# Strassen's seven half-size products for the down matmul of tiles 1 to 8, and column halves for attention, in a fused attention and feed-forward kernel

## The chip, the cores and the metric

The kernel runs on one core of one Trainium2 chip. The metric is device microseconds (us) of one execution. TensorE is called PE in the profile, its weight loads PEld, VectorE DVE, ScalarE ACT, GpSimd POOL, and SyncE SP. "Matmul of 256 columns" means that the moving operand has 256 columns.

Ratios are the mean time of one kernel's fast runs over the mean of the other's fast runs of the same rounds, so they are not quite the ratio of the medians that stand beside them. A run counts as slow when it is over 1.5% above the fastest of the same kernel, and is left out of the ratios. The granted clock is the share of TensorE's full clock rate that the trace says it was given.

## The reference

```python
# q, k, v: (8 batches, 8 heads, 576 positions, 64); pool = 8
k_p, v_p = mean of k, v over groups of 8 positions      # 72 keys per head
attn = softmax(q @ k_p.T / 8)                           # 576 x 72
x = (attn @ v_p), heads side by side                    # 4608 tokens x 512
h = x @ w_in                                            # 512 -> 2048, "up"
out = (h * cos(h)) @ w_out                              # 2048 -> 512, "down", float32
```

## The kernel before

Tokens go in nine tiles (0 to 8) of 512. A tile has an up stage (64 matmuls, with a cosine on ACT and a multiplication on DVE) and a down stage (64 matmuls of 512 columns). The attention of batch t + 1 is woven into the down stage of tile t, at fixed positions in the list of matmuls. It goes in units of four heads by 256 positions; the last 64 positions of a batch, for all eight heads, are "the rest". `obank` are the two PSUM banks that the down stage writes, `bank` three pairs of banks for the up stage and attention. POOL sums groups of eight keys and values for batches 2 to 7, in the down stages of tiles 1 to 5 and, for batch 2, around the end of tile 0.

Values and row sums of the softmax come out of one full-width matmul, because the weights hold 64 columns of values and 64 of ones:

```python
def values(b, u, pair, later=None):
    ...
    for i in range(nh):
        pj, hp = divmod(h0 + i, 2)
        nc.tensor.matmul(pair[:, hp, (i // 2) * n:(i // 2 + 1) * n],
                         lhsT=vz[b % 2][:, pj, 2 * hp:2 * hp + 2, :].rearrange("p a d -> p (a d)"),
                         rhs=ex[:, ex_col(u, i):ex_col(u, i) + n])
    ...                                            # Ln on 64 partitions, twice
    nc.scalar.activation(out=inv, in_=lnc, func=ACTF.Exp, scale=-1.0)
    ...                                            # tensor_mul on 64 partitions, twice

def down_mm(o, ms, fc):
    nc.tensor.matmul(o, lhsT=g_sb[:, fc, ms * 128:(ms + 1) * 128],
                     rhs=w_out_sb[fc // 4][:, fc % 4, :], start=(fc == 0), stop=(fc == FFCH - 1))

def pool_add(b, which):
    ...
    add = nc.gpsimd.tensor_tensor
    add(out=s, in0=x[:, :, 0:4, :], in1=x[:, :, 4:8, :], op=ADD)                      # 4.06 us
    add(out=s[:, :, 0:2, :], in0=s[:, :, 0:2, :], in1=s[:, :, 2:4, :], op=ADD)        # 2.35 us
    ...
```

The last 128 rows of tile 8 are done in pieces of 256, 128 and 128 columns (`last_chunk`), so that little is left after the last matmul.

The softmax here doesn't subtract the row's maximum and nothing guards it: scores larger than these inputs give would overflow.

## Time and profile before

The median of three runs was 302.38 us (302.17 to 302.52), the span of the profile 301.4 us.

| stage (from matmul starts in the trace) | us |
|---|---|
| up stage, tiles 1 to 8, each | 13.85 |
| down stage, tiles 1 to 6, each | 17.45 |
| down stage, tile 7, tile 8 | 14.41, 13.84 |
| last matmul's start to the end of the span | 3.71 |

PE is never idle from tile 0 to the last matmul, so each stage is as long as its matmuls. (A stage runs from its first matmul's start to the next stage's; tile 8's down stage to its last matmul's start.) The lines that show it stand in the prediction. In a line of a group, the columns are line, engine, operation, tiles, shapes and count, then busy time and the mean of one in ns, then the engine's idle time just before it and what ended it.

### The profile page before, as it was taken

What the parts mean: (1) busy time and instruction counts of PE and PEld (TensorE: products, weight loads), DVE (VectorE), ACT (ScalarE), POOL (GpSimd) and SP (SyncE); (2) the same over time, 40 slices, a digit from 0 to 9 for tenths busy, and PEclk for the clock granted to TensorE, in tenths of its full rate; (3) what the DMA queues carried; (4) which work ended last, traced back from release to release, by engine and by line L of the source; (5) the groups of instructions that cost most, each with busy time, mean ns of one, the idle gap of its engine ahead of it and who ended that gap; (6) DMA issues with size and microseconds to landing.
All of it is one profiled execution on the core that took longest, in us unless ns stands there. A gap on an engine that the chain in (4) does not pass through costs nothing.

```text
span 301.4 us, 4625 instructions
## 1 busy us (share of the span) xinstructions
PE 293.9 (97%) x1816; PEld 143.2 (48%) x1816; DVE 170.8 (57%) x212; ACT 205.7 (68%) x254; POOL 130.4 (43%) x93
## 2 busy tenths in 40 slices
PE   8789999999999999999999999999999999999995
PEld 3445544445544454445444544455444544444444
DVE  5448637465467446754666556654775477425712
ACT  3786798469876987688778886789668966605500
POOL 8463016984983398239913990389300000000000
PEclk9999999999999999999999999999999999999999
DMA  7999999639526961697079617791811130131023
GB/s 152 197 207 206 206 205 195 141 55 176 117 60 124 167 127 29 146 158 140 6 170 143 129 36 171 94 174 39 141 32 35 37 70 0 37 70 35 0 67 75
DMA packets 44165, 32.91 MB, mean 109 GB/s; under 512 B 22128, under 2 KB 39408, under 8 KB 44144
## 3 DMA queue, kind: packets, MB, share of 16 engines
q0 software_dynamic: 19744, 18.07, 38.3%
q1 hardware_dynamic: 24160, 14.42, 20.5%
q8 instruction: 14, 0.23, 0.3%
q10 hardware_dynamic: 240, 0.13, 0.2%
q14 instruction: 7, 0.06, 0.1%
HBM read 36.70 MB, written 9.44 MB: 153 GB/s over the span
## 4 chain that ended last, share of the span: by engine, by line
PE 93%; DMA 4%; POOL 1%; DVE 1%; issue 0%; POOLq 0%; DVEq 0%
PE bank L297 41%; PE obank L310 41%; PE bank L241 5%; DMA kv_st<-in_v_dram 4%; PE bank L211 3%; PE bank L328 1%; PE bank L165 1%; POOL q_b L84 1%; PE obank L157 0%; PE obank L280 0%; PE obank L192 0%; DVE xT L282 0%; DVE vz L167 0%; POOL kv_st L84 0%; DVE o_sb L316 0%
## 5 line engine op out<-in xcount | busy, mean ns | idle before, releaser
L310 PE MATMUL obank<-w_out_sb,g_sb 128*128 128x512 bf16 x560 | 131.4, 379 | 0.0
L297 PE MATMUL bank<-xT,w_in_sb 128*128 128x512 bf16 x576 | 126.6, 379 | 0.0
L304 ACT ACTIVATE cos<-bank,half_pi 128x1024 f32<-128x1024 f32 x72 | 79.3, 1113 | 59.5 <-PE bank L297 59.5
L307 DVE TENSOR_TENSOR g_sb<-bank,cos 128x1024 bf16<-128x1024 f32 x72 | 87.3, 1223 | 43.0 <-ACT cos L304 42.9
L297 PEld LDWEIGHTS <-w_in_sb 128*128 128x128 bf16 x576 | 56.1, 98 | 67.6 <-issue 1.6
L310 PEld LDWEIGHTS <-g_sb 128*128 128x128 bf16 x560 | 52.8, 98 | 56.5 <-issue 2.0
L252 DVE TENSOR_TENSOR xT<-bank,inv 64x512 bf16<-64x512 f32 (+1 forms) x72 | 45.3, 629 | 40.8 <-ACT inv L248 40.1
L141 POOL TENSOR_TENSOR kv_st<-kv_st 72x2048 f32<-72x2048 bf16 x12 | 48.7, 4058 | 33.9 <-DMA kv_st<-in_k_dram 33.9
L247 ACT ACTIVATE lnc<-bank 64x512 f32<-64x512 f32 (+1 forms) x72 | 39.2, 544 | 3.1 <-PE bank L241 1.7
L316 DVE COPY o_sb<-obank 128x512 f32<-128x512 f32 x35 | 23.6, 689 | 30.9 <-PE obank L310 30.5
L218 ACT ACTIVATE ex<-bank 72x1024 bf16<-72x1024 f32 (+1 forms) x40 | 35.0, 929 | 8.5 <-PE bank L211 8.4
L142 POOL TENSOR_TENSOR kv_st<-kv_st 72x1024 f32<-72x1024 f32 x12 | 28.2, 2349 | 1.0
L248 ACT ACTIVATE inv<-lnc 128x512 f32<-128x512 f32 (+1 forms) x36 | 21.0, 583 | 1.1
L241 PE MATMUL bank<-ex,vz 72*128 72x256 bf16 (+1 forms) x176 | 20.0, 243 | 0.0
L241 PEld LDWEIGHTS <-vz 72*128 72x128 bf16 x176 | 13.6, 97 | 9.6 <-DVE xT L252 0.5
L145 POOL TENSOR_TENSOR kp<-kv_st 72x512 bf16<-72x512 f32 x12 | 14.9, 1263 | 0.5
L211 PE MATMUL bank<-qT,kk 64*72 64x256 bf16 (+1 forms) x192 | 13.2, 252 | 0.0
L211 PEld LDWEIGHTS <-kk 64*72 64x72 bf16 x192 | 7.4, 109 | 9.9 <-issue 7.2
L285 ACT ACT_TABLE_LOAD x9 | 11.5, 1283 | 0.9 <-PEq L519 0.7
L499 POOL COPY gate<-kk 1x1 bf16<-1x1 bf16 x5 | 0.9, 179 | 25.7 <-DMA kk<-kp 25.7
L288 ACT ACT_TABLE_LOAD x9 | 11.5, 1283 | 0.2
L103 POOL DMA_DIRECT2D kv_st<-in_v_dram x6 | 5.0, 841 | 8.8 <-PE bank L165 8.8
(55 smaller groups left out, 93.1 us busy)
## 6 DMA issues: line engine op xcount, KB each, us to landing
out_dram<-o_sb SPq DMA_DIRECT2D x70, 128.0 KB, 2.4
kv_st<-in_v_dram POOLq DMA_DIRECT2D x8, 576.0 KB, 13.7
kv_st<-in_k_dram POOLq DMA_DIRECT2D x7, 576.0 KB, 7.6
q_b<-in_q_dram POOLq DMA_DIRECT2D x6, 576.0 KB, 9.9
w_in_sb<-in_moe_w_in_dram POOLq DMA_DIRECT2D x4, 512.0 KB, 14.5
w_out_sb<-in_moe_w_out_dram POOLq DMA_DIRECT2D x4, 512.0 KB, 18.1
q_b<-in_q_dram POOLq DMA_DIRECT2D x4, 288.0 KB, 13.0
g_sb<-in_k_dram SPq DMA_DIRECT2D x1, 576.0 KB, 3.7
```

Source lines behind the costliest of these rows:

```text
L141: add(out=s, in0=x[:, :, 0:4, :], in1=x[:, :, 4:8, :], op=ADD)
L142: add(out=s[:, :, 0:2, :], in0=s[:, :, 0:2, :], in1=s[:, :, 2:4, :], op=ADD)
L211: nc.tensor.matmul(pair[:Sp, bank, c:c + n].rearrange("p (g n) -> p g n", n=64), lhsT=kk[b % 2][half[r], h0 + i, 0:Sp], rhs=att["qT", b][h ...
L218: nc.scalar.activation(out=ex[:, 0:nh * n].rearrange("p (a n) -> p a n", a=2), in_=pair[:Sp, :, 0:nh * n // 2], func=ACTF.Exp, scale=scale ...
L241: nc.tensor.matmul(pair[:, hp, (i // 2) * n:(i // 2 + 1) * n], lhsT=vz[b % 2][:, pj, 2 * hp:2 * hp + 2, :].rearrange("p a d -> p (a d)"), ...
L247: nc.scalar.activation(out=lnc[half[1 - hp]], in_=pair[half[1 - hp], hp, 0:w], func=ACTF.Ln)
L252: nc.vector.tensor_mul(out=x_out(b, u, half[hp]), in0=cols(pair[half[hp], hp, :], u), in1=cols(inv[half[1 - hp]], u))
L297: nc.tensor.matmul(h[:, j, :], lhsT=w_in_sb[fc // 4][:, ki, (fc % 4) * 128:(fc % 4 + 1) * 128], rhs=xT[:, ki, t * TILE:(t + 1) * TILE], st ...
L304: nc.scalar.activation(out=cos, in_=h, func=ACTF.Sin, bias=half_pi[:, :1])
L307: nc.vector.tensor_mul(out=g_sb[:, 2 * fp:2 * fp + 2, :], in0=h, in1=cos)
L310: nc.tensor.matmul(o, lhsT=g_sb[:, fc, ms * 128:(ms + 1) * 128], rhs=w_out_sb[fc // 4][:, fc % 4, :], start=(fc == 0), stop=(fc == FFCH - 1))
L316: nc.vector.tensor_copy(out=o[:, 0:n], in_=ps)
```

## The change

The intent is fewer columns on PE. Tokens, the 2048 inner features and the 512 outputs are each cut in half, and Strassen's scheme gives the four output blocks from seven products instead of eight. A tile's down stage has 7 x 16 = 112 matmuls of 256 columns instead of 64 of 512. The price is sums: of `g` in every tile (`gs`, `gx`, `gd`), of the weights once after tile 0, and of the products. The column halves of attention put row sums and values of two heads into the two 64-column halves of the array, so that logarithm and multiplication need one instruction on 128 partitions each instead of two on 64; that is to make room on ACT and DVE.

```diff
 def pool_add(b, which):
-        add(out=s, in0=x[:, :, 0:4, :], in1=x[:, :, 4:8, :], op=ADD)
-        add(out=s[:, :, 0:2, :], in0=s[:, :, 0:2, :], in1=s[:, :, 2:4, :], op=ADD)
+        for h in range(0, H, 2):
+            add(out=s[:, h:h + 2], in0=x[:, h:h + 2, 0:4, :], in1=x[:, h:h + 2, 4:8, :], op=ADD)
+        for h in range(0, H, 4):
+            add(out=s[:, h:h + 4, 0:2, :], in0=s[:, h:h + 4, 0:2, :], in1=s[:, h:h + 4, 2:4, :], op=ADD)
 def values(b, u, pair, later=None):
...
+        cs, ao = pair[:, 0, 0:w], pair[:, 1, 0:w]
+        for out_of, weights in ((cs, lambda i: ones[:Sp, :]),
+                                (ao, lambda i: vz[b % 2][:, (h0 + i) // 2, i % 2, :])):
+            for i in range(nh):
+                hp = i % 2
+                nc.tensor.matmul(out_of[hp * 64:hp * 64 + 64, (i // 2) * n:(i // 2 + 1) * n], lhsT=weights(i),
+                                 rhs=ex[:, ex_col(u, i):ex_col(u, i) + n])
...
+    def put_weights():              # wx = B11 + B22, wy = B11 + B12, wz = -(B21 + B22), two parts each
+    def put_weights_in_place():     # B12 -= B22, B21 -= B11 (as w_out_sb then stands), two parts each
+    def put_gs(fp): ...             # behind every second up_g; gx and gd behind the products
...
+        products = [
+            (1, True, False, sides(g_sb, 0, 0), of(w_out_sb[0:2], 1)),
+            (0, True, False, sides(g_sb, 1, 1), of(w_out_sb[2:4], 0)),
+            (1, False, True, sides(gs, 0, 0), of(w_out_sb[2:4], 1)),
+            (0, False, True, sides(gs, 0, 1), of(w_out_sb[0:2], 0)),
+            (1, True, False, sides(gx, 0, 0), of(wx, 0)),
+            (0, True, True, sides(gd, 1, 0), of(wz, 0)),
+            (1, False, True, sides(gd, 0, 0), of(wy, 0)),
+        ]                            # the first entry is the output bank; False, True adds into it
...
+        behind = {n: [m3, *gxs[0:1]], 2 * n: [m4, *gxs[1:]], 3 * n: [c12, *gds[0:2]], 4 * n: [c21, *gds[2:]],
+                  5 * n: [m1], 6 * n: [c11], 7 * n: [c22]}          # n = 16 matmuls
...
+            if t == 1:
+                for put in put_weights_in_place():
+                    put()
...
+            for put in put_weights():          # after tile 0's down stage
+                put()
```

Left out are buffers that share space to make room, the order of the up matmuls (first and second half of the features in turn) and the positions of attention among 112 matmuls; in tile 7 the values of the rest stay at position 16.

More of the change, by code (lines that the diff above doesn't have):

```diff
@@ L64 @@
     g_sb = wpool.tile([128, FFCH, TILE], BF16, name="g_sb")
+    HF, HT, HM = FFCH // 2, TILE // 2, d_model // 2
+    gs = wpool.tile([128, HF, TILE], BF16, name="gs")
+    gd = wpool.tile([128, FFCH, HT], BF16, name="gd")
+    gx = wpool.tile([128, HF, HT], BF16, name="gx")
+    wx = [wpool.tile([128, 4, HM], BF16, name=f"wx{i}") for i in range(2)]
+    wy = [wpool.tile([128, 4, HM], BF16, name=f"wy{i}") for i in range(2)]
+    wz = [wpool.tile([128, 4, HM], BF16, name=f"wz{i}") for i in range(2)]
     SpA = -(-Sp // 16) * 16
@@ L68 @@
     kp2 = [wpool.tile([SpA, H, 2, D], BF16, name=f"kp2{i}") for i in range(2)]
-    vz = [wpool.tile([Sp, KCH, 4, D], BF16, name=f"vz{i}") for i in range(2)]
+    vz = [wpool.tile([Sp, KCH, 2, D], BF16, name=f"vz{i}") for i in range(2)]
+    half_sums = wpool.tile([Sp, H, POOL // 2, D], FP32, name="half_sums")
     banks = [psum.tile([128, 2, 512], FP32, name=f"bank{i}") for i in range(3)]
@@ L86, in kv_tile @@
     def kv_tile():
-        return kvst.tile([128, 2 * H * POOL * D], BF16, name="kv_st", tag="kv_st")
+        return kvst.tile([128, 2 * KCH * ROW * D], BF16, name="kv_st", tag="kv_st")
     def even_part(st, i):
@@ L100, in load_kv @@
     def load_kv(b, which, src):
-        st = kv_tile()[:Sp].rearrange("p (i h t d) -> p i h t d", i=2, h=H, t=POOL)
-        nc.gpsimd.dma_start(out=st[:, 0].rearrange("p h t d -> p h (t d)"),
+        st = kv_tile()[:Sp, 0:H * POOL * D].rearrange("p (h t d) -> p h t d", h=H, t=POOL)
+        nc.gpsimd.dma_start(out=st.rearrange("p h t d -> p h (t d)"),
                             in_=src[b].rearrange("h (p t) d -> p h (t d)", t=POOL))
@@ L125, in v_part @@
     def v_part(b):
-        return vz[b % 2][:, :, 0:4:3, :]
+        return vz[b % 2]
     def put_kk(b, ps, pj0, pj1, copy):
@@ L136, in pool_add @@
         st = staged.pop((which, b))
-        x = st[:, 0]
-        s = st[:, 1].rearrange("p h t d -> p (h t d)").bitcast(FP32).rearrange(
-            "p (h t d) -> p h t d", h=H, t=POOL // 2)
+        x, s = st, half_sums
         add = nc.gpsimd.tensor_tensor
-        add(out=s, in0=x[:, :, 0:4, :], in1=x[:, :, 4:8, :], op=ADD)
-        add(out=s[:, :, 0:2, :], in0=s[:, :, 0:2, :], in1=s[:, :, 2:4, :], op=ADD)
+        for h in range(0, H, 2):
+            add(out=s[:, h:h + 2], in0=x[:, h:h + 2, 0:4, :], in1=x[:, h:h + 2, 4:8, :], op=ADD)
+        for h in range(0, H, 4):
+            add(out=s[:, h:h + 4, 0:2, :], in0=s[:, h:h + 4, 0:2, :], in1=s[:, h:h + 4, 2:4, :], op=ADD)
         if which == "k":
@@ L230, in inverse_tile @@
     def inverse_tile(w):
-        lnc = asb.tile([128, 512], FP32, name="lnc", tag="lnc", bufs=1)
         inv = asb.tile([128, 512], FP32, name="inv", tag="inv", bufs=3)
-        return lnc[:, 0:w], inv[:, 0:w]
+        return inv[:, 0:w], inv[:, 0:w]
     def values(b, u, pair, later=None):
@@ L238, in values @@
         ex = att.pop(("ex", b, u))
-        for i in range(nh):
-            pj, hp = divmod(h0 + i, 2)
-            nc.tensor.matmul(pair[:, hp, (i // 2) * n:(i // 2 + 1) * n],
-                             lhsT=vz[b % 2][:, pj, 2 * hp:2 * hp + 2, :].rearrange("p a d -> p (a d)"),
-                             rhs=ex[:, ex_col(u, i):ex_col(u, i) + n])
-        w = nh * n // 2
+        w = nh * n // 2
+        cs, ao = pair[:, 0, 0:w], pair[:, 1, 0:w]
[5 more added lines that the diff above has]
+                                 rhs=ex[:, ex_col(u, i):ex_col(u, i) + n])
         lnc, inv = inverse_tile(w)
-        for hp in range(2):
-            nc.scalar.activation(out=lnc[half[1 - hp]], in_=pair[half[1 - hp], hp, 0:w], func=ACTF.Ln)
+        nc.scalar.activation(out=lnc, in_=cs, func=ACTF.Ln)
         nc.scalar.activation(out=inv, in_=lnc, func=ACTF.Exp, scale=-1.0)
         def mul():
-            for hp in range(2):
-                nc.vector.tensor_mul(out=x_out(b, u, half[hp]), in0=cols(pair[half[hp], hp, :], u),
-                                     in1=cols(inv[half[1 - hp]], u))
+            nc.vector.tensor_mul(out=x_out(b, u, slice(0, 128)), in0=cols(ao, u), in1=cols(inv, u))
         if later is None:
@@ L280, in values_then @@
             nc.tensor.matmul(ao[hp * 64:hp * 64 + 64, (i // 2) * n:(i // 2 + 1) * n],
-                             lhsT=vz[b % 2][:, pj, 3 * hp, :], rhs=ex[:, ex_col(u, i):ex_col(u, i) + n])
+                             lhsT=vz[b % 2][:, pj, hp, :], rhs=ex[:, ex_col(u, i):ex_col(u, i) + n])
         nc.vector.tensor_mul(out=x_out(b, u, slice(0, 128)), in0=cols(ao, u), in1=cols(att.pop(("inv", b, u)), u))
@@ L288, in sin_tables, with up_order, up_bank @@
         nc.scalar.preload_act_table_set("trig_and_small")
+    def up_order(t):
+        n = FFCH // 2
+        return range(n) if t == 0 else [i + a * n // 2 for i in range(n // 2) for a in range(2)]
+    def up_bank(t, fp):
+        return banks[list(up_order(t)).index(fp) % 3]
     def up_mm(t, fp, k0=0, k1=KCH):
-        h = banks[fp % 3]
+        h = up_bank(t, fp)
         for j in range(2):
@@ L301, in up_g @@
     def up_g(t, fp, between=()):
-        h = banks[fp % 3]
+        h = up_bank(t, fp)
         cos = msb.tile([128, 2, TILE], FP32, name="cos", tag="cos", bufs=2)
@@ L311, in down_mm, with down_out @@
                          rhs=w_out_sb[fc // 4][:, fc % 4, :], start=(fc == 0), stop=(fc == FFCH - 1))
-    def down_out(t, ms, ps, c0=0, queues=(nc.sync, nc.sync)):
-        o = msb.tile([128, d_model], FP32, name="o_sb", tag="o_sb", bufs=6)
-        n = ps.shape[1]
-        nc.vector.tensor_copy(out=o[:, 0:n], in_=ps)
+    def down_out(t, ms, ps):
+        o = msb.tile([128, 2, d_model], FP32, name="o_two", tag="o_two", bufs=3)[:, 0]
+        nc.vector.tensor_copy(out=o, in_=ps)
         rows_of = out.rearrange("(b p t) m -> b t p m", b=B, t=ROW)
@@ L319, in down_out @@
             b_, pos = divmod((t * TILE + ms * 128) // 64 + i, ROW)
-            queues[i].dma_start(out=rows_of[b_, ORDER[pos], :, c0:c0 + n], in_=o[rows, 0:n])
-    def last_chunk():
-        t, ms = NT - 1, 3
-        for i, (c0, n) in enumerate(((0, 256), (256, 128), (384, 128))):
-            ps = banks[i][:, 0, 0:n]
-            for fc in range(FFCH):
-                nc.tensor.matmul(ps, lhsT=g_sb[:, fc, ms * 128:(ms + 1) * 128],
-                                 rhs=w_out_sb[fc // 4][:, fc % 4, c0:c0 + n],
-                                 start=(fc == 0), stop=(fc == FFCH - 1))
-            down_out(t, ms, ps, c0, (nc.sync, nc.scalar))
@@ L334 @@
-    EX = 5
-    warm = consts.tile([128, 512], BF16, name="warm")
+            nc.sync.dma_start(out=rows_of[b_, ORDER[pos]], in_=o[rows])
+    def put_weights():
+        mul, sub = mybir.AluOpType.mult, mybir.AluOpType.subtract
+        for i in range(2):
+            (b11, b12), (b21, b22) = [(w[:, :, 0:HM], w[:, :, HM:]) for w in (w_out_sb[i], w_out_sb[i + 2])]
+            yield lambda i=i, x=b11, y=b22: nc.vector.tensor_tensor(out=wx[i], in0=x, in1=y, op=ADD)
+            yield lambda i=i, x=b11, y=b12: nc.vector.tensor_tensor(out=wy[i], in0=x, in1=y, op=ADD)
+            yield lambda i=i, x=b21, y=b22: nc.vector.scalar_tensor_tensor(out=wz[i], in0=x, scalar=-1.0, in1=y,
+                                                                          op0=mul, op1=sub)
@@ new lines, in put_weights_in_place @@
+    def put_weights_in_place():
+        sub = mybir.AluOpType.subtract
+        for i in range(2):
+            w1, w2 = w_out_sb[i], w_out_sb[i + 2]
+            yield lambda w1=w1, w2=w2: nc.vector.tensor_tensor(out=w1[:, :, HM:], in0=w1[:, :, HM:],
+                                                               in1=w2[:, :, HM:], op=sub)
+            yield lambda w1=w1, w2=w2: nc.vector.tensor_tensor(out=w2[:, :, 0:HM], in0=w2[:, :, 0:HM],
+                                                               in1=w1[:, :, 0:HM], op=sub)
@@ new lines, in put_gs, with put_gx, put_gd @@
+    def put_gs(fp):
+        f = slice(2 * fp, 2 * fp + 2)
+        nc.vector.tensor_tensor(out=gs[:, f], in0=g_sb[:, f], in1=g_sb[:, HF + 2 * fp:HF + 2 * fp + 2], op=ADD)
+    def put_gx(i):
+        f = slice(4 * i, 4 * i + 4)
+        nc.vector.tensor_tensor(out=gx[:, f], in0=g_sb[:, f, 0:HT], in1=g_sb[:, HF + 4 * i:HF + 4 * i + 4, HT:], op=ADD)
+    def put_gd(i):
+        f = slice(4 * i, 4 * i + 4)
+        nc.vector.tensor_tensor(out=gd[:, f], in0=g_sb[:, f, HT:], in1=g_sb[:, f, 0:HT], op=mybir.AluOpType.subtract)
@@ new lines, in down_products, with of, sides, m3 @@
+    def down_products(t):
+        def of(w, m):
+            return lambda fc: w[fc // 4][:, fc % 4, m * HM:(m + 1) * HM]
+        def sides(x, f, tk):
+            return lambda fc, p: x[:, f * HF + fc, tk * HT + p * 128:tk * HT + (p + 1) * 128]
+        products = [
[7 more added lines that the diff above has]
+        ]
+        mms = []
+        for bank, first, last, g, w in products:
+            for fc in range(HF):
+                for p in range(2):
+                    mms.append(lambda bank=bank, first=first, last=last, g=g, w=w, fc=fc, p=p: nc.tensor.matmul(
+                        obanks[bank][:, p * HM:(p + 1) * HM], lhsT=g(fc, p), rhs=w(fc),
+                        start=(first and fc == 0 and p == 0), stop=(fc == HF - 1 and p == 1), skip_group_check=not first))
+        e = msb.tile([128, d_model], FP32, name="e_sb", tag="e_sb", bufs=1)
+        u = msb.tile([128, d_model], FP32, name="u_sb", tag="u_sb", bufs=1)
+        os = [msb.tile([128, 2, d_model], FP32, name="o_two", tag="o_two", bufs=3) for _ in range(2)]
+        two = lambda x: x.rearrange("p (a m) -> p a m", a=2)
+        vec = nc.vector.tensor_tensor
+        sub = mybir.AluOpType.subtract
+        def m3():
+            nc.scalar.copy(out=e, in_=obanks[1])
+        def m4():
+            vec(out=e, in0=obanks[0], in1=e, op=ADD)
+        def c12():
+            nc.scalar.copy(out=os[0][:, :, HM:], in_=two(obanks[1]))
+            vec(out=u, in0=e, in1=obanks[1], op=sub)
+        def c21():
+            nc.scalar.copy(out=os[1][:, :, 0:HM], in_=two(obanks[0]))
+            vec(out=e, in0=e, in1=obanks[0], op=sub)
+        def m1():
+            vec(out=u, in0=obanks[1], in1=u, op=ADD)
+        def c11():
+            vec(out=os[0][:, :, 0:HM], in0=two(obanks[0]), in1=two(u), op=ADD)
+            rows_out(t, 0, os[0])
+        def c22():
+            vec(out=os[1][:, :, HM:], in0=two(obanks[1]), in1=two(e), op=ADD)
+            rows_out(t, 1, os[1])
+        gxs = [lambda i=i: put_gx(i) for i in range(2)]
+        gds = [lambda i=i: put_gd(i) for i in (2, 3, 0, 1)]
+        n = 2 * HF
+        behind = {n: [m3, *gxs[0:1]], 2 * n: [m4, *gxs[1:]], 3 * n: [c12, *gds[0:2]], 4 * n: [c21, *gds[2:]],
+                  5 * n: [m1], 6 * n: [c11], 7 * n: [c22]}
+        return mms, behind
@@ L336, with rows_out @@
+    def rows_out(t, tk, o):
+        rows_of = out.rearrange("(b p t) m -> b t p m", b=B, t=ROW)
+        for p in range(2):
+            for i, rows in enumerate(half):
+                b_, pos = divmod((t * TILE + tk * HT + p * 128) // 64 + i, ROW)
+                nc.sync.dma_start(out=rows_of[b_, ORDER[pos]], in_=o[rows, p])
+    EX = 4
+    warm = gx.rearrange("p f n -> p (f n)")[:, 0:512]
     nc.vector.memset(warm, 1.0)
@@ L357 @@
     make_identity(nc, identity)
-    dist = consts.tile([128, ROW, Sp], FP32, name="dist")
-    sign = consts.tile([128, ROW, Sp], FP32, name="sign")
-    groups = consts.tile([128, ROW, Sp], BF16, name="groups")
+    dist, sign = [gs.rearrange("p f n -> p (f n)").bitcast(FP32)[:, i * 1024:i * 1024 + ROW * Sp].rearrange(
+        "p (t n) -> p t n", t=ROW) for i in range(2)]
+    groups = gd.rearrange("p f n -> p (f n)")[:, 0:ROW * Sp].rearrange("p (t n) -> p t n", t=ROW)
     nc.vector.tensor_tensor(out=dist, in0=row_of.unsqueeze(2).to_broadcast([128, ROW, Sp]),
@@ L365 @@
     nc.vector.tensor_scalar(out=groups, in0=sign, scalar1=0.0, scalar2=None, op0=mybir.AluOpType.is_le)
-    nc.vector.memset(vz[0], float(POOL))
     ones = consts.tile([128, D], BF16, name="ones")
@@ L382 @@
     load_even(staged["v", 1], 1, v)
-    nc.gpsimd.memset(vz[1], float(POOL))
     for i in range(2):
@@ L427 @@
         if t > 0:
-            up_mm(t, 0, 0, 2)
-            up_mm(t, 1, 0, 2)
-        for fp in range(FFCH // 2):
-            up_mm(t, fp, 2 if fp < 2 else 0)
+            for fp in up_order(t)[0:2]:
+                up_mm(t, fp, 0, 2)
+            if t == 1:
+                for put in put_weights_in_place():
+                    put()
+        for n, fp in enumerate(up_order(t)):
+            up_mm(t, fp, 2 if n < 2 else 0)
             between = ()
@@ L443 @@
             up_g(t, fp, between)
+            if 0 < t and n % 2:
+                put_gs(n // 2)
             if 0 < t and b < B:
-                if fp == 0:
+                if n == 0:
                     q_transpose(b)
-                elif fp == 2:
+                elif n == 2:
                     k_transpose(b)
@@ L480, in scores_of @@
                 return go
-            fill = [(4, scores_of((b, us[0], 2), (b, us[1], 0))), (14, V_(0, 1, later)), (16, lambda: later.pop()()),
-                    (19, V_(1, 2)), (35, scores_of((b, us[2], 0), (b, us[3], 1), (t, REST, 2))),
-                    (38, V_(2, 0)), (43, lambda: values(t, REST, banks[1])), (46, V_(3, 2))]
+            fill = [(6, scores_of((b, us[0], 2), (b, us[1], 0))), (27, V_(0, 1, later)), (32, lambda: later.pop()()),
+                    (35, V_(1, 2)), (61, scores_of((b, us[2], 0), (b, us[3], 1), (t, REST, 2))),
+                    (67, V_(2, 0)), (76, lambda: values(t, REST, banks[1])), (82, V_(3, 2))]
         fi = 0
-        if t == NT - 1:
-            mms = mms[:-FFCH]
-        for n, (ms, fc) in enumerate(mms):
-            while fi < len(fill) and fill[fi][0] <= n:
-                fill[fi][1]()
-                fi += 1
-            down_mm(obanks[ms % 2], ms, fc)
-            if fc == FFCH - 1:
-                down_out(t, ms, obanks[ms % 2])
+        if t == 0:
+            for n, (ms, fc) in enumerate(mms):
+                while fi < len(fill) and fill[fi][0] <= n:
+                    fill[fi][1]()
+                    fi += 1
+                down_mm(obanks[ms % 2], ms, fc)
+                if fc == FFCH - 1:
+                    down_out(t, ms, obanks[ms % 2])
+            for put in put_weights():
+                put()
+        else:
+            mms, behind = down_products(t)
+            for n, mm in enumerate(mms):
+                for go in behind.get(n, ()):
+                    go()
+                while fi < len(fill) and fill[fi][0] <= n:
+                    fill[fi][1]()
+                    fi += 1
+                mm()
+            for go in behind[len(mms)]:
+                go()
         if t < B:
@@ L505 @@
             pool_add(b + 1, "v")
-    last_chunk()
 _INS = ['q', 'k', 'v', 'moe_w_in', 'moe_w_out']
```

## The prediction

No number of the sum goes with them: parts 1 to 6 come to +7.6 us, about 310, and 2 for contention with POOL make 312.

"Drain" is used below for the gap of 0.09 to 0.10 us that the prediction measures between matmuls on 128*128 and those on 64*72 or 72*64; what the array does in it was not shown.

> **What bounds the kernel now.** I read the page first (busy shares, then the chain that ended last), then the chain piece by piece, then short timelines of one tile.
>
> ```profile
> PE 293.9 (97%) x1816; PEld 143.2 (48%) x1816; DVE 170.8 (57%) x212; ACT 205.7 (68%) x254; POOL 130.4 (43%) x93
> PE 93%; DMA 4%; POOL 1%; DVE 1%; issue 0%; POOLq 0%; DVEq 0%
> L310 PE MATMUL obank<-w_out_sb,g_sb 128*128 128x512 bf16 x560 | 131.4, 379 | 0.0
> L297 PE MATMUL bank<-xT,w_in_sb 128*128 128x512 bf16 x576 | 126.6, 379 | 0.0
> L252 DVE TENSOR_TENSOR xT<-bank,inv 64x512 bf16<-64x512 f32 (+1 forms) x72 | 45.3, 629 | 40.8 <-ACT inv L248 40.1
> L247 ACT ACTIVATE lnc<-bank 64x512 f32<-64x512 f32 (+1 forms) x72 | 39.2, 544 | 3.1 <-PE bank L241 1.7
> ```
>
> TensorE (PE) carries 93% of the chain; up (L297) and down (L310) matmuls have no idle time before them. The two groups that the column halves shorten, Ln (L247) and the multiplication (L252), have slack: their engines are at 68% and 57%. So only a shorter PE stream, or a new wait on it, moves the time. The chain in order of time shows one tile (tile 2, from 85.46):
>
> ```profile
> 85.46 13.84 PE bank L297 x64
> 99.30 0.86 PE obank L310 x4
> 100.16 0.56 PE bank L211 x8
> ...
> 102.99 0.45 PE bank L241 x4
> ...
> 112.86 3.89 PE obank L310 x18
> 116.75 13.85 PE bank L297 x64
> ...
> 294.40 3.55 PE bank L328 x48
> ```
>
> Sixty-four matmuls of 512 columns take 13.84 us: 0.216 us each. Up plus down plus attention is 31.3 us a tile with no gap. The last line is the final chunk, 16 matmuls of 256 columns and 32 of 128, 3.55 us; its own starts are 0.109 and 0.056 us apart, so a new weight load of 128 columns hides even behind these short ones.
>
> [...]
>
> ```profile
> 99.35 0.81 PE L310 MATMUL obank<-w_out_sb,g_sb 128*128 128x512 bf16 x3
> 100.09 0.30 PE L211 MATMUL bank<-qT,kk 64*72 64x256 bf16 x2
> ...
> 12.19 0.41 PE L266 MATMUL obank<-ex,ones 72*64 72x256 bf16 x4 [0.15 <-DVE kk L132]
> 12.54 0.39 PE L392 MATMUL bank<-warm 128*128 128x512 bf16 x1
> ```
>
> The third matmul of the first line starts at 99.785, so a stream would go on at 100.00; the scores start at 100.09: 0.09 us. The column-half sums (L266) end their stream at 12.44 (last start 12.33 plus 0.107), the next full matmul starts at 12.53: 0.10 us. Within the mode a pair of halves takes 0.108 us, the first pair 0.03 more. [...] By analogy with L316 (128x512 f32, 0.69 us) I estimate a 1024-column bf16 sum at 0.69 us, 0.61 when it overlaps its predecessor (back-to-back L316 start 0.61 apart).
>
> **The change part by part.**
> 1. Down matmul: 64 x 0.216 = 13.81 us becomes 7 products x 8 x 2 = 112 matmuls of 256 columns x 0.109 = 12.23 us. Saved: 1.58 us in each of tiles 1 to 7; in tile 8, 48 x 0.216 + 3.55 - 12.23 = 1.68. Sum -12.8 us.
> 2. Column halves: a values unit is 4 x 0.109 = 0.44 us now. After it is 8 halves = 4 pairs, 0.43 + 0.03, plus 0.09 in and 0.10 out = 0.65: +0.21. The rest unit (8 x 64 columns) about +0.23. Four units and a rest in tiles 1 to 6: +1.07 each, 6.4; tile 0 about +1.0 (its rest follows another row-tiled group); tile 7 +0.23. Sum +7.6 us. Ln and multiplication halve on ACT and DVE, off the path.
> 3. The sums of the weights: ten DVE instructions between tile 0's last eviction (54.20 + 0.69 = 54.89, 0.73 after PE's end at 54.16) and tile 1's first multiplication by the cosine. At 0.61 to 0.69, perhaps 1.2 for the two three-operand ones: 6.3 to 7.4 us. DVE comes to that multiplication at 61.2 to 62.3, not 57.9. PE has three banks, so it stands when the fourth pair needs bank 0, at 54.16 + 3 x 1.73 = 59.35, and goes on 1.2 us after the multiplication starts, at 62.5 to 63.5. Sum about +3.5 us.
> 4. The end: the last product leaves a 128x512 combination (0.69 us against 0.29) and four output issues one after the other on one queue, at about 0.52 us each, behind the four of the other half; before, two small issues on two queues. Last matmul start to end of span is now 297.72 to 301.4, 3.7 us; I work out 6.4. Sum +2.75 us.
> 5. Waits in the down stage of tiles 1 to 6. Count from its start T (tile 2: 99.14).
>  - ACT: cosine to T+1.4, table load to 2.6, two exps to 3.65 and 4.56 (from 101.76 and 102.69 of tile 2). The new copy of product 1's bank stands behind them and ends at 5.15. PE reaches product 3, which adds into that bank, at 32 x 0.109 + 0.65 (scores) + 0.65 (values) + 0.1 = T+4.85: waits 0.3.
>  - Product 4's bank is copied by ACT behind three exps of scores that start at T+9.2: these take 2.87 us from the scores' start (108.34 to 111.20), so the copy ends at 12.6 and DVE's subtraction behind it at 13.4. PE wants that bank for product 6 at 13.2: 0.2.
>  - DVE, held by that subtraction with nothing running from about 10.7, then has two of the differences of g, two multiplications and the addition of product 5, which must be done before product 7 uses the bank: T+16.2 against T+15.8: 0.4.
>  Sum 0.9 x 6 = +5.4 us. In tile 7 the rest values stay at position 16, now T+2.1, but their exp ends at T+3.25 (258.25 + 0.59, T = 255.62): +1.15.
> 6. The new DVE sums in the up stage: 8 x 1.22 + 4 x 0.69 = 12.5 us of 13.8; fits.
>
> PE stream -12.8 + 7.6 = -5.2; plus 3.5 + 2.75 + 5.4 + 1.15 = +12.8. Net +7.6: about 310.
>
> **Rivals.**
> - *POOL contention.* POOL's sums run right through the down stage in tiles 1 to 5 and through the weight sums:
>
> ```profile
> 102.76 4.06 POOL L141 TENSOR_TENSOR kv_st<-kv_st 72x2048 f32<-72x2048 bf16 x1 [5.48 <-DMA kv_st<-in_k_dram]
> 106.91 2.35 POOL L142 TENSOR_TENSOR kv_st<-kv_st 72x1024 f32<-72x1024 f32 x1
> 109.34 2.49 POOL L145 TENSOR_TENSOR kp<-kv_st 72x512 bf16<-72x512 f32 x2
> 111.79 4.06 POOL L141 TENSOR_TENSOR kv_st<-kv_st 72x2048 f32<-72x2048 bf16 x1
> ```
>
>  The change cuts L141 into four and L142 into two, some 1.0 to 1.2 us each[...]. If DVE waits once per burst (about 0.55 us): product 7's wait grows by 0.5 in five tiles and the weights by 0.5, +3: 313. If the engines alternate, each DVE sum waits 1.1 us: product 7 waits 1.6 more in five tiles and the weights up to 7 more, +15: 325. I add 2 to the middle.
> - *The waits are absorbed.* If ACT and DVE come 0.5 us earlier than I laid out in a chain of a dozen steps, part 5 falls to 1 or 2 us: about 305. For it: the positions 27, 32 and 61 look fitted to when the exps end.
> - *The full saving comes through* (12.8 us, 4%, time 291). Against it: drains of 0.09 and 0.10 us are in the trace, as is the three-bank limit on a late DVE.
>
> **Range and chances.** Middle 310 + 2 = 312. Low end 304: parts 1 to 4 alone give 303.5. High end 322: contention between the two forms. Faster by over 2% needs under 296.3, below what parts 1 to 4 allow: 0.03. Within 2% ends at 308.4 and needs most of part 5 to vanish: 0.27. Slower: 0.70.
>
> **What would show it.** Right: starts of down matmuls 0.109 us apart in tiles 1 to 8; attention units of about 0.65 us; PE idle of 3 us or more, released by DVE's cosine multiplication, once after tile 0; PE waits before products 3, 6 and 7 in tiles 1 to 6, released by ACT's copy and DVE's subtraction and addition; bf16 sums longer than 0.69 us wherever POOL adds. Wrong: PE still without idle in tiles 1 to 6 (part 5 falls), a start spacing over 0.109 (weight loads not hidden), or bf16 sums near 1.2 us everywhere[...].

## The result, and the profile after

The changed kernel took 328.44 us median (327.24 to 328.64, 4 runs), beside 302.45 us (302.17 to 302.70) before: ratio 1.0849, 95% interval 1.0828 to 1.0869. It is slower by 26 us, outside the predicted range of 304 to 322.

| stage | before | after | difference |
|---|---|---|---|
| start to the end of tile 0 | 54.0 | 54.3 | +0.3 |
| tile 1, up | 13.85 | 27.72 | +13.9 |
| tile 1, down | 17.45 | 19.49 | +2.0 |
| tiles 2 to 5, down | 17.45 each | 19.06, 18.93, 19.72, 19.36 | +7.3 |
| tile 6, down | 17.45 | 17.59 | +0.1 |
| tile 7, down | 14.41 | 14.13 | -0.3 |
| tile 8, down | 13.84 | 12.12 | -1.7 |
| up stages of tiles 2 to 8 | 13.85 each | 13.84 each | 0 |
| last matmul to the end | 3.71 | 7.16 | +3.4 |

The page of the changed kernel, in the lines that answer to those shown of before:

```profile
PE 293.6 (90%) x2344; PEld 177.9 (55%) x2344; DVE 237.6 (73%) x279; ACT 196.3 (60%) x242; POOL 152.6 (47%) x140
PEclk9999999758999999999999999999999999999998
PE 24%; ACT 2%; DVE 1%; issue 1%; ACTq 0%
L314 PE MATMUL bank<-xT,w_in_sb 128*128 128x512 bf16 x576 | 128.9, 383 | 11.6 <-DVE g_sb L324 11.6
L367 DVE TENSOR_TENSOR gd<-g_sb 128x1024 bf16<-128x1024 bf16 x32 | 36.3, 1174 | 0.0
L359 DVE TENSOR_TENSOR gs<-g_sb 128x1024 bf16<-128x1024 bf16 x32 | 23.1, 721 | 1.1
L390 PE MATMUL obank<-wy,gd 128*128 128x256 bf16 x128 | 15.3, 272 | 9.6 <-DVE u_sb L416 9.6
```

PE's share fell from 97% to 90% and DVE's rose from 57% to 73%. PE now has two idle groups, both released by DVE: 11.6 us in the up matmuls and 9.6 us before product 7 (the one with `wy` and `gd`). The clock line, granted clock in 40 slices, dips in slices 8 to 10. The chain's shares add up to under 30% of the span (it was followed back no further than 231 us), so here it isn't the place to look. The two groups of bf16 sums are of one shape, yet `gs` takes 721 ns and `gd` 1174.

The 11.6 us, in the timeline of tile 1 (start, length, engine, line, tiles, count):

```profile
54.28 5.34 PE L314 MATMUL bank<-xT,w_in_sb 128*128 128x512 bf16 x24
71.19 10.98 PE L314 MATMUL bank<-xT,w_in_sb 128*128 128x512 bf16 x40 [11.57 <-DVE g_sb L324]
...
55.09 1.41 DVE L343 TENSOR_TENSOR wx<-w_out_sb,w_out_sb 128x1024 bf16<-128x1024 bf16 x1
56.42 1.64 DVE L344 TENSOR_TENSOR wy<-w_out_sb 128x1024 bf16<-128x1024 bf16 x1
57.98 2.17 DVE L345 SCALAR_TENSOR_TENSOR wz<-w_out_sb 128x1024 bf16<-128x1024 bf16 x1
...
69.32 0.68 DVE L354 TENSOR_TENSOR w_out_sb<-w_out_sb,w_out_sb 128x1024 bf16<-128x1024 bf16 x1
69.92 2.34 DVE L324 TENSOR_TENSOR g_sb<-bank,cos 128x1024 bf16<-128x1024 f32 x2
...
56.02 6.69 POOL L152 TENSOR_TENSOR half_sums<-kv_st 72x512 f32<-72x512 bf16 x4
62.67 3.90 POOL L154 TENSOR_TENSOR half_sums<-half_sums 72x512 f32<-72x512 f32 x2
```

PE fills its three banks with 24 matmuls and stands until the multiplication at 69.92. Before it, DVE works off the ten weight sums. Those that meet POOL's sums last 1.4 to 2.3 us, the last one, which meets none, 0.68. The granted clock, taken from windows of the trace, falls to 0.50 from 62 us on and is back at 1.00 only from 76 us: the 40 matmuls behind the gap begin at half speed (from 72 to 74 us 6 of them ran, from 76 to 78 us 11). POOL is slowed too: four pieces in 6.69 us, 1.67 each, where an undisturbed one takes 1.15.

And before product 7, in tile 2 (DVE and PE):

```profile
128.32 2.76 DVE L367 TENSOR_TENSOR gd<-g_sb 128x1024 bf16<-128x1024 bf16 x2
131.94 0.67 DVE L416 TENSOR_TENSOR u_sb<-obank,u_sb 128x512 f32<-128x512 f32 x1
...
132.66 0.71 PE L390 MATMUL obank<-wy,gd 128*128 128x256 bf16 x5 [1.64 <-DVE u_sb L416]
```

Two differences of `g` take 2.76 us; the addition that frees the bank comes behind them, and PE waits for it. (Two multiplications of attention stand between them, 131.00 to 131.94.)

### The profile page after: what moved, and what is told of

Same layout as the page of the kernel before. It is cut to its first block, busy times and chain, and to the rows that moved or that the text cites. A ratio compares the mean times of both kernels' runs of the same rounds, so it can differ in the third digit from the quotient of the medians.

```text
span 326.5 us, 5776 instructions
## 1 busy us (share of the span) xinstructions
PE 293.6 (90%) x2344; PEld 177.9 (55%) x2344; DVE 237.6 (73%) x279; ACT 196.3 (60%) x242; POOL 152.6 (47%) x140
## 5 line engine op out<-in xcount | busy, mean ns | idle before, releaser
L314 PE MATMUL bank<-xT,w_in_sb 128*128 128x512 bf16 x576 | 128.9, 383 | 11.6 <-DVE g_sb L324 11.6
L152 POOL TENSOR_TENSOR half_sums<-kv_st 72x512 f32<-72x512 bf16 x48 | 60.9, 1296 | 35.1 <-DMA kv_st<-in_k_dram 34.7
L367 DVE TENSOR_TENSOR gd<-g_sb 128x1024 bf16<-128x1024 bf16 x32 | 36.3, 1174 | 0.0
L154 POOL TENSOR_TENSOR half_sums<-half_sums 72x512 f32<-72x512 f32 x24 | 34.5, 1458 | 0.0
L390 PEld LDWEIGHTS <-gd 128*128 128x128 bf16 x256 | 24.5, 98 | 15.3 <-issue 11.8
L390 PE MATMUL obank<-w_out_sb,g_sb 128*128 128x256 bf16 x256 | 31.7, 273 | 0.0
L390 PE MATMUL obank<-w_out_sb,gs 128*128 128x256 bf16 x256 | 31.3, 273 | 0.2
L390 PEld LDWEIGHTS <-g_sb 128*128 128x128 bf16 x256 | 23.9, 98 | 6.6 <-issue 2.4
L390 PEld LDWEIGHTS <-gs 128*128 128x128 bf16 x256 | 24.1, 98 | 5.2 <-issue 2.4
L359 DVE TENSOR_TENSOR gs<-g_sb 128x1024 bf16<-128x1024 bf16 x32 | 23.1, 721 | 1.1
L327 PE MATMUL obank<-w_out_sb,g_sb 128*128 128x512 bf16 x64 | 15.7, 380 | 0.6 <-DMA w_out_sb<-in_moe_w_out_dram 0.6
## 6 DMA issues: line engine op xcount, KB each, us to landing
q_b<-in_q_dram POOLq DMA_DIRECT2D x4, 288.0 KB, 12.7
```

Source lines behind the costliest of these rows:

```text
L152: add(out=s[:, h:h + 2], in0=x[:, h:h + 2, 0:4, :], in1=x[:, h:h + 2, 4:8, :], op=ADD)
L154: add(out=s[:, h:h + 4, 0:2, :], in0=s[:, h:h + 4, 0:2, :], in1=s[:, h:h + 4, 2:4, :], op=ADD)
L314: nc.tensor.matmul(h[:, j, :], lhsT=w_in_sb[fc // 4][:, ki, (fc % 4) * 128:(fc % 4 + 1) * 128], rhs=xT[:, ki, t * TILE:(t + 1) * TILE], st ...
L359: nc.vector.tensor_tensor(out=gs[:, f], in0=g_sb[:, f], in1=g_sb[:, HF + 2 * fp:HF + 2 * fp + 2], op=ADD)
L367: nc.vector.tensor_tensor(out=gd[:, f], in0=g_sb[:, f, HT:], in1=g_sb[:, f, 0:HT], op=mybir.AluOpType.subtract)
L390: mms.append(lambda bank=bank, first=first, last=last, g=g, w=w, fc=fc, p=p: nc.tensor.matmul(obanks[bank][:, p * HM:(p + 1) * HM], lhsT=g ...
```

## The experiments

Theory L: VectorE's sums with two SBUF inputs and GpSimd's sums take turns, one whole instruction each. Rival W: the order of ScalarE's and VectorE's work in the down stage causes the waits, with or without GpSimd. Rival M: bf16 sums are slow by themselves, because of their strides. Beside these stand the lowered clock, and the prediction's own terms for the drains and the end.

### 1. Without GpSimd's sums (e1_no_pool_sums, wrong result)

```diff
 def pool_add(b, which):
-        st = staged.pop((which, b))
-        ...                          # all of GpSimd's sums
+        staged.pop((which, b))
+        return
```

> The changed kernel without GpSimd's sums for the pooled keys and values (wrong result on purpose; loads and everything else stay). Theory L[...]: VectorE's sums with two SBUF inputs and GpSimd's sums take turns, so without GpSimd's sums every bf16 sum on VectorE takes about 0.68 us, the down stages of tiles 1 to 5 fall from 18.9 to 19.7 us to tile 6's 17.6, and the up stage of tile 1 from 27.7 to about 18 us; in all some 18 us less, near 310. Rival W, the order of ScalarE's and VectorE's work in the down stage alone: down stages of tiles 1 to 5 stay at 19 us and only tile 1's up stage shortens, near 318. Rival M, bf16 sums slow by themselves because of their strides: nothing changes, 328.

Measured: 311.03 us (308.74 to 312.51) beside 301.90, ratio 1.0285 (1.0233 to 1.0338). The timeline around tile 1's start, and below it a line of the groups:

```profile
55.19 0.68 DVE L342 TENSOR_TENSOR wx<-w_out_sb,w_out_sb 128x1024 bf16<-128x1024 bf16 x1
56.39 1.22 DVE L344 SCALAR_TENSOR_TENSOR wz<-w_out_sb 128x1024 bf16<-128x1024 bf16 x1
63.53 10.48 PE L313 MATMUL bank<-xT,w_in_sb 128*128 128x512 bf16 x40 [3.81 <-DVE g_sb L323]
```

```profile
L366 DVE TENSOR_TENSOR gd<-g_sb 128x1024 bf16<-128x1024 bf16 x32 | 20.6, 684 | 0.0
```

The same sums with the same strides take 0.68 us without GpSimd, so rival M falls. (In the changed kernel VectorE's sums with both inputs in SBUF grow beside GpSimd, `gs`, `gx` and `gd` from 0.68 or 0.69 to as much as 1.48, 1.75 and 1.76 us; the 72 multiplications with an input in PSUM took 1.21 to 1.225 us throughout.) The down stages of tiles 1 to 6 are all 17.59 us, so rival W falls as the cause of the excess in tiles 1 to 5. Nor is it that GpSimd's results come late: behind tile 0 the changed kernel's trace has PE wait for DVE (11.6 and 9.6 us) and for an exp of ACT (1.0 us), for nothing of GpSimd's. Tile 1's up stage is 19.47 us: PE still stands for 3.81 us behind the ten sums. Against the changed kernel this is 17 us less (1.0849 against 1.0285 of 302).

### 2. Without the weight sums (e2_no_weight_sums and e2b_no_weight_sums, wrong results on purpose)

```diff
-                for put in put_weights_in_place():
-                    put()
+                pass
...
-            for put in put_weights():
-                put()
...
+    for x in (*wx, *wy, *wz):
+        nc.vector.memset(x, 0.01)    # e2b: nc.gpsimd.memset, after the loads of w_out
```

> The changed kernel without the ten sums of the weights (constant tiles in their place, wrong result on purpose). If the whole excess of tile 1's up stage (27.7 against 13.8 us) hangs on these ten sums: 13.9 us less, near 314.5, with no TensorE idle time and no lower clock after tile 0; all down stages unchanged. If part of the excess has another cause, such as the first matmuls of tile 1 waiting for attention, tile 1's up stage stays over 14.5 us.

Measured: 317.32 us, fast runs 315.79 to 317.53 beside 301.90, ratio 1.0483 (1.0446 to 1.0520); one run, the profiled one, was slow. Tile 1's up stage was 13.84 us. But the first up matmul of that trace started at 22.6 us instead of 17.2, most likely because VectorE set my six constant tiles at the start. So I ran it again with that mended.

> The run without the ten weight sums again, with the constant tiles set by GpSimd after the weight loads are issued instead of by VectorE at the start, where they delayed the first stage by 5 us (wrong result on purpose). If tile 1's up stage returns to 13.84 us and nothing else changes: 13.9 us less than the changed kernel, near 314.5. The excess of this run over the one with neither sums (305.3) is then [...]in the down stages of tiles 1 to 5 alone, some 9 us.

Measured: 312.70 us (312.58 to 313.66) beside 302.21, ratio 1.0352 (1.0334 to 1.0370). Tile 1's up stage is 13.85 us, and the down stages of tiles 1 to 5 are 18.87, 18.67, 19.06, 19.34 and 19.40 us, together 1.2 us shorter than in the changed kernel. The run is 1.8 us faster than expected, but the whole excess of tile 1's up stage hangs on the ten sums.

### 3. Without either (e5_neither, wrong result)

Both edits together.

> The changed kernel without GpSimd's sums and without the weight sums (constant tiles, set by GpSimd while it is idle; wrong result on purpose). The run without GpSimd's sums kept a stall of 5.6 us in tile 1's up stage (19.47 against 13.85 us); [...]this run is 5.6 us faster than that one: near 305.4, still slower than before by the drains and the end less the saving. Rival: some of what was left in tile 1 is not the weight sums: its up stage stays over 14.5 us.

Measured: 305.31 us (304.73 to 306.12) beside 302.26, ratio 1.0103 (1.0088 to 1.0119), as expected; tile 1's up stage is 13.85 us and each down stage of tiles 1 to 6 is 17.59. The four runs make a square:

| ratio to before | with weight sums | without |
|---|---|---|
| with GpSimd's sums | 1.0849 | 1.0352 |
| without | 1.0285 | 1.0103 |

The weight sums cost 15.0 us of 302 where GpSimd sums too and 5.5 us where it doesn't. GpSimd's sums cost 7.5 us in the down stages alone (1.0352 less 1.0103), near the 9 us expected: a little less. The 1.0% that is left is the rest of the change without either: its saving does not pay for its drains, waits and end.

### 4. Keeping TensorE busy in the gap (e3_keep_warm)

```diff
+            if t == 1 and n == 3:
+                for i in range(50):
+                    nc.tensor.matmul(obanks[0], lhsT=w_in_sb[0][:, 0, 0:128], rhs=w_in_sb[0][:, 1, :])
```

> The changed kernel with 50 idle matmuls on TensorE in the gap of tile 1's up stage (10.8 us of the 11.6 us gap), so that its clock is not lowered. If the lowered clock after the gap costs what the trace suggests (the 40 matmuls after the gap took 10.81 us where 8.64 is their full-speed time): 2.2 us less, 326.2, and granted clock 1.00 from 62 to 75 us. If the clock is not the reason for their slowness (VectorE's late multiplications instead): no change, 328.4.

Measured: 327.47 us (325.86 to 329.66) beside 301.90, ratio 1.0841 (1.0778 to 1.0903), result correct. In the timeline of this run:

```profile
59.19 10.95 PE L541 MATMUL obank<-w_in_sb 128*128 128x512 bf16 x50
71.53 8.79 PE L314 MATMUL bank<-xT,w_in_sb 128*128 128x512 bf16 x40 [1.38 <-DVE g_sb L324]
```

The granted clock was 1.00 from 62 to 75 us. The 40 matmuls after the gap took 8.63 us from first start to the next stage, 10.81 in the changed kernel: the lowered clock did slow them, by 2.2 us. The time of the whole kernel doesn't show it beyond its scatter: the interval holds the changed kernel's 1.0849, and 2.2 us less (1.0776) lies just below its end. The trace shows why so little came of it. The matmuls after the gap started 0.6 us later after the stage's start than in the changed kernel, so that tile 1's up stage was 1.6 us shorter (26.14 against 27.72); and the clock was lowered elsewhere, to 0.50 from 230.9 to 234.3 us, where product 7 of tile 5 took 2.44 us instead of 1.74 and tile 6's up stage 14.83 instead of 13.85.

### 5. The column halves alone (e4_halves_only)

`values` and `vz` of the changed kernel in the kernel before, nothing else.

> The kernel before with the column halves for attention alone, no Strassen. My prediction's part 2: two drains per unit of values on a full TensorE, +7.6 us, near 310. Rival: the halves cost nothing because they relieve ScalarE and VectorE: 302.4. If the halves cost less than a drain of 0.09 to 0.10 us each way per unit, between the two.

Measured: 309.13 us (308.99 to 309.60) beside 301.90, ratio 1.0232 (1.0209 to 1.0254), 7.2 us by the medians. Each down stage of tiles 1 to 6 grew from 17.45 to 18.48 us. PE has no idle time there: the drains cost what was predicted.

### 6. The changed kernel with full-width values (e6_full_width)

`values` and `vz` of the kernel before in the changed one (and two buffers of `inv` instead of three, for space).

> The changed kernel with the values of the kernel before (full width, no drains; one buffer of the inverse less, for space). If the drains are the main cost of the second half of the change, 7 us less: 321. If the halves are there to make room on VectorE and ScalarE (two multiplications and two logarithms per unit again, some 3 us more on each per down stage, which the wait before product 7 feels), the down stages of tiles 1 to 6 grow by 1 to 2 us net: 334 to 340.

Measured: 349.38 us (348.15 to 350.24) beside 302.26, ratio 1.1546 (1.1526 to 1.1566). The direction is that of the second reading, the size was missed by 9 us. The down stages of tiles 1 to 5 are 23.1 to 23.8 us; in tile 2's, DVE is busy for 20.64 of 23.72 us and PE for 18.09. So the halves do make the room that they are there for, most of all beside GpSimd; in tile 6, where GpSimd sums nothing, the down stage is 18.85 us against 17.59 with the halves. (One buffer less is part of this run, and its share was not tested.) Most of the 9 us is a lowered clock: in the down stages of tiles 1 to 5 PE waits some 3.5 us before product 7, the granted clock is then 0.50 for 3.4 us, and product 7 takes 3.1 to 3.3 us instead of the changed kernel's 1.74, 7.6 us in all.

### 7. GpSimd's sums uncut (e8_uncut)

```diff
-        for h in range(0, H, 2):
-            add(out=s[:, h:h + 2], ...)
-        for h in range(0, H, 4):
-            add(out=s[:, h:h + 4, 0:2, :], ...)
+        add(out=s, in0=x[:, :, 0:4, :], in1=x[:, :, 4:8, :], op=ADD)
+        add(out=s[:, :, 0:2, :], in0=s[:, :, 0:2, :], in1=s[:, :, 2:4, :], op=ADD)
```

> The changed kernel with GpSimd's sums in one piece each as before (4.06 and 2.35 us instead of pieces of 1.15 to 1.2). If the loser[...] waits for the whole instruction of the other, VectorE's sums of g take up to 4.7 us where they meet the long ones, and the waits before product 7 grow: 332 to 338, with tile 1's up stage about as long as now, since the same GpSimd work lies in front. [...]

Measured: 351.53 us, fast runs 351.09 to 351.55 beside 302.26, ratio 1.1625 (1.1609 to 1.1642); the fourth run, the profiled one, was slow (356.83). The `gd` sums of the changed kernel and, below, of this run (shortest, median, longest in ns):

```profile
L367 DVE TENSOR_TENSOR gd<-g_sb x32: 683/1025/1761, 91.1 to 316.3; 128x1024 bf16<-128x1024 bf16 x32
L365 DVE TENSOR_TENSOR gd<-g_sb x32: 677/866/4537, 94.3 to 344.8; 128x1024 bf16<-128x1024 bf16 x32
```

The longest took 4.54 us, 0.68 plus nearly the whole 4.06 of the uncut sum, and the down stages of tiles 1 to 5 took 23.0 to 26.5 us in this slow run, while tile 1's up stage was about as long as in the changed kernel (28.2 against 27.7). So a short sum waited for as good as the whole of a long one. I expected 332 to 338 (and 328 if the sizes made no difference); the fast runs are 23 us above the changed kernel. Not all of that is this waiting directly. The mean granted clock of the fast runs is 0.951, of the changed kernel's 0.975; at a granted clock of 0.50 while it was lowered, as in the windows read above, that is some 34 us of 350 against 16 of 326, so I estimate that up to 9 of the 23 us are the lowered clock behind the longer waits.

### 8. Strassen where nothing meets it (e7_two_tiles and e9_two_tiles_mended)

From these findings I built a version on the kernel before, with full-width values: Strassen in tiles 7 and 8 alone, where GpSimd sums nothing. The weight sums go into tile 6's down stage, into columns of `xT` that are no longer read; nothing is done in place.

```diff
+        if t == FIRST - 1:                                   # FIRST = 7
+            fill += zip((2, 6, 10, 22, 24, 28, 30, 48, 50, 52), put_weights())
...
+        if t >= FIRST:
+            fill = [(1, fill[0][1]), (34, fill[1][1])] if fill else []
+            mms, behind = down_products(t)
```

> A version built from the findings: the kernel before, with Strassen in tiles 7 and 8 alone, where GpSimd sums nothing and attention is over; full-width values; the ten weight sums spread over tile 6's down stage, where VectorE has slack and GpSimd is idle; the last tile's last product in two banks, its outputs in column halves on two queues. Saving 1.58 us in tile 7 and 1.68 in tile 8, the end about 0.6 us longer: 2.7 us less than before, near 299.7 (ratio 0.991). If something of the Strassen down stage still waits without GpSimd and attention, it is near 302.4.

Measured: 301.78 us (301.05 to 305.60, 6 runs, the longest of them slow) beside 302.26, ratio 0.9985 (0.9965 to 1.0005), result correct: 0.5 us less, where 2.7 were expected. Waits of 1.4 us explain more than half of what was missing; the rest I did not follow, and the interval is 1.2 us wide. The timelines of PE and DVE in tile 7 show one part:

```profile
246.98 1.24 PE L304 MATMUL bank<-xT,w_in_sb 128*128 128x512 bf16 x5 [0.56 <-DVE g_sb L314]
...
243.98 1.22 DVE L351 SCALAR_TENSOR_TENSOR xT<-w_out_sb 128x1024 bf16<-128x1024 bf16 x1
```

Tile 7 starts at 241.08, and the last weight sum is still running at 245.2; the next up matmul starts 0.72 us later than at full rate (the line's 0.56 counts from the modelled end of the matmul before). The other part was 0.68 us in tile 8: the last product's second half waited for DVE's read of the first half's bank, though it writes another bank of the same tile.

```diff
-            fill += zip((2, 6, 10, 22, 24, 28, 30, 48, 50, 52), put_weights())
+            fill += zip((2, 3, 5, 6, 8, 10, 20, 22, 24, 26), put_weights())
...
-        split = [banks[0][:, p, 0:HM] for p in range(2)]
+        split = [banks[p][:, 0, 0:HM] for p in range(2)]
```

(The last tile also got a third output buffer.)

> The version with Strassen in tiles 7 and 8 alone, mended where its trace showed TensorE waiting: the weight sums come earlier in tile 6 (the last three ran into tile 7's up stage, 0.72 us), and the last product's two halves are in two separately declared tiles of PSUM (the second half waited 0.68 us for the first's combination though it lay in another bank). Both waits gone: 1.4 us less than that version, near 300.0, ratio to before about 0.993. If the waits only move: 301.5.

Measured: 300.41 us (300.29 to 301.12) beside 302.21, ratio 0.9939 (0.9926 to 0.9952), result correct, both waits gone; a new one of 0.54 us stands before a group of scores in tile 6, put down to a multiplication of DVE (`xT`, L252), which comes there behind six weight sums in a row. It makes tile 6's down stage 0.4 us longer (17.86 against 17.45); that the new places of the weight sums cause it was not tested. The end is 1.3 us longer than before (5.00 against 3.72), where 0.6 was reckoned. This version beats the kernel before by 0.6%, clear of noise, and the changed kernel by 8%.

## Why the prediction was wrong

The direction was right, slower with a chance of 0.70, and the size was not: 328.4 us where the range ended at 322.

**Part 1, the saving.** Right: tile 8, which has neither attention nor GpSimd, went from 13.84 to 12.12 us between first and last start; with the last matmul's own 0.056 and 0.109 us that is 1.67 less, where 1.68 was predicted.

**Part 2, the drains.** Right: +7.2 us measured alone, +7.6 predicted.

**Part 3, the weight sums.** The mechanism, three banks and a late multiplication, is what the trace shows. Without GpSimd PE stood 3.81 us (predicted 3.5), but the stage grew by 5.6 us: the matmuls after the gap were slow, and 40 of them took 10.32 us instead of 8.64. That is the lowered clock, which no part of my sum had. Experiment 4 shows its cost for the longer gap; for this one only the granted clock says so, 0.54 in the 2.5 us behind the gap.

**Part 4, the end.** Mechanism right, size a little off: the last matmul's start to the end is 7.16 us, predicted 6.4. The eight output issues took 4.96 us in a row, 0.62 each, where some 0.52 was reckoned (in the trace before they take 0.47 to 1.33, median 0.58); that is about the difference.

**Part 5, the waits in the down stage.** Right: without GpSimd a down stage is 17.59 us. The kernel before's 17.45, plus 1.03 for the drains, less 1.61 saved (64 x 0.216 less 112 x 0.109), is 16.87; that leaves 0.7 us for the waits, predicted 0.9. The starts in tile 2 of experiment 3 show them at the places predicted: 0.20 us before product 3 (predicted 0.3), 0.12 before product 6 (0.2) and 0.33 before product 7 (0.4). (The prediction's sum for product 3, T+4.85, is 4.89 from its own terms, and part 1 adds up to 12.7; neither matters.) Tile 7's wait was 1.16 us, predicted 1.15.

**Part 6, the up stage.** Right from tile 2 on: 13.84 us.

**The step that failed** is the first rival, "POOL contention", and what I did with it: "I add 2 to the middle." I reckoned with the contention, without a trace that showed it, and worked out both forms, once per burst (+3) and in alternation (+15), gave the middle less than the mild one, and ended the range at 322, below the alternation's 325. The runs show the alternation: GpSimd's sums add 17 us, of which tile 1's up stage has 8.25 (27.72 less 19.47; up to 7 reckoned) and the down stages of tiles 1 to 5 have 8.6 (their sum, 96.6, less 5 x 17.59; 8 reckoned). The middle of 310 plus 15 is 325, and the lowered clock's 2.2 us in the changed kernel brings it to 327. The term that was missing altogether is this lowered clock. I had read the cutting of GpSimd's sums as a sign that its author had met such waits; experiment 7 shows that the cutting makes them less costly, the longest `gd` sum 1.76 us against 4.54, and doesn't remove them.

**The rival of absorbed waits** fell: part 5's waits are there in each of tiles 1 to 6. **The rival of the full saving** fell with the drains.

**The steps that stood on cut passages.** That the two engines hold each other up: a `gd` sum takes 0.68 us without GpSimd, up to 1.76 beside the cut sums and 4.54 beside the uncut ones (experiments 1 and 7). The order at one bank: in the changed kernel's tile 2, DVE's subtraction starts at 127.71, after ACT's copy of the same bank from 127.10 to 127.68, though it needs nothing of the copy; the trace puts its wait of 1.22 us down to the copy. Whether the bank or a semaphore of the program enforces the order was not shown. The bf16 sum: 0.68 us where 0.69 was estimated.

## What to carry to other kernels

Where VectorE's sums with both inputs in SBUF and GpSimd's sums both have full queues, take as the first estimate that every short one waits for a whole one of the other side, and count what stands behind it: here a sum of 0.68 us took up to 1.76 us beside pieces of 1.15 to 1.27, and up to 4.54 beside one of 4.06. A saving on the bounding engine can be lost to drains and to waits on another engine's new work, as the 12.8 us were here: place one-time preparation where both the engine and its neighbours have slack, then look for where it spills over. Reckon with a lowered clock behind an idle gap on TensorE: here the matmuls behind gaps of 3.8 and 11.6 us took 1.7 and 2.2 us more. Behind the waits of 1.6 to 2.5 us in the changed kernel's down stages they did not (product 7 took 1.74 us in each), but behind one of 2.3 us in experiment 4 they did.

## What was measured of single instructions

- With both queues full, VectorE's sums with both inputs in SBUF and GpSimd's sums alternated: the weight sums, 0.68 to 1.22 us each alone, took 1.4 to 2.3 us while GpSimd worked. The profile has this waiting in the busy time of the instruction (1174 ns mean for a `gd` sum, 684 without GpSimd).
- The drain is 0.09 to 0.10 us in each direction, and the first pair of halves takes 0.03 us more (the changed kernel, tile 2: the halves start at 119.11 where the products' stream would have gone on at 119.01, and the products at 119.67 where the halves ended at 119.58).
- In bf16, `scalar_tensor_tensor` took 1.22 us for 1024 columns, `tensor_tensor` 0.68 (experiment 1).
- Streams with a fresh weight load for each matmul ran at 56 ns a matmul at 128 columns (32 matmuls at the end of the kernel before), 109 at 256 and 216 at 512.
